# A first balancing round with its row maximum subtracted and 1e-9 added to its column sums

## The chip, the core and the metric

The kernel runs on one core of one Trainium2 chip. The metric is the device time of one execution in microseconds (us). A core has five engines that run their own instruction lists and wait for one another by semaphores: TensorE (PE in the profile, its weight loads PEld), VectorE (DVE), ScalarE (ACT), GpSimd (POOL) and SyncE (SP). Transfers between the device memory and the core's SBUF run on 16 DMA engines and are issued by SyncE, ScalarE or GpSimd.

## The reference

Attention over blocks with a learned order of the blocks, and then a two-branch feed-forward. What matters here is the head: a matrix of 8 x 8 for each of 4 batches and 8 heads is balanced in five rounds (Sinkhorn), and mixes the blocks of k and v.

```python
P = sort_net                                   # [4, 8, 8, 8]
for _ in range(5):
    P = P - np.max(P, axis=-1, keepdims=True)
    P = np.exp(P)
    P = P / (np.sum(P, axis=-1, keepdims=True) + 1e-09)
    P = P / (np.sum(P, axis=-2, keepdims=True) + 1e-09)
...
k_sorted = np.einsum('bhij,bhjcd->bhicd', P, k_b)
v_sorted = np.einsum('bhij,bhjcd->bhicd', P, v_b)
...   # scores within each block of 96 rows, softmax, times v_sorted -> x [3072, 512]
h1 = x @ w1
h2 = x @ w2
out = np.maximum(h1, h2) @ w_out               # [3072, 512]
```

The sequence has 768 rows, the head dimension is 64, w1 and w2 are 512 x 1024, w_out is 1024 x 512; the inputs and the output are float32.

## The kernel before

**The list of steps.** The whole work of four batches is written as a list of short tokens, which is read from left to right and emits instructions (`token`, L1081, and `plan`, L1176). Each engine executes its own instructions in that order, so the list is a schedule made by hand: a step that waits on an engine holds back everything that stands later in the list on the same engine. The list begins

```
lw1 lw2 I1 lk0.0 lk0.1 lk0.2 lq0.0 lq0.1 lq0.2 S0 m0 S1 m1 S2 m2 tv0.18A S3 tv18.36A lq0.3
J1 S4 m3 tv36.56A tv56.80A D0 ...
```

`lw`, `lk` and `lq` issue loads of v, k and q from GpSimd; `I1` makes the identity `ident` on GpSimd; `S0` to `S4` are the five balancing rounds; `m0` to `m2` make masks on VectorE between the rounds and `m3` copies them on GpSimd; `tv` turns v on ScalarE; `J1` makes selection matrices on GpSimd (`one_j`, `sel_v`), as `g1` to `g3` do (`sel_k`, `sel_v`); `D0` spreads the balanced matrix over the partitions (`block_diagonals_first`, L357).

**The rounds.** `sort_net` is loaded by SyncE into `p_sb`, 32 partitions (batch x head) of 8 x 8 float32 (L115). A round, `sinkhorn` (L269), is one Exp on ScalarE in place (L270) and six VectorE instructions in place: row sums into `rowsum` (L276), their reciprocal (L277), a product with the reciprocal spread along the row (L278), column sums into `colsum` (L281), their reciprocal (L282), and the product (L283), which in the last round writes `p_bf` in bfloat16. There is no maximum and no 1e-9 in any of the five rounds. Each instruction needs the one before it.

**TensorE meanwhile.** From the start TensorE multiplies zeros (`keep_streaming`, L78): 92 matmuls of 118 columns (L1079). In rounds 3 and 4 it multiplies zeros again, six matmuls of 512 columns each, with weights `late` that VectorE sets to zero in that round behind the round before it (`late_zeros`, L86 to L88), so that these matmuls start with the round. 

**Behind the rounds.** `D0` is nine small matmuls with `p_bf` (L361, L368); with their results VectorE makes the block-diagonal weights `bd` (L376 to L393), with which TensorE sorts k (L489) and v (L510) of batch 0. Then come scores (L584), Exp (L599), values (L612), and the feed-forward, which is computed by block sums and differences (`sums_x`, `sums_g`, L891, L907; products at L805 and L961), with the later batches' attention in between. `x` is turned by DMA transposes from SBUF to SBUF for batches 1 to 3 (L642). Loads for the later batches and the weights are issued by GpSimd in the order of the list.

Of the kernel before, what the change touches and what calls it, by code (L numbers as in the profile page):

```python
# [16 lines left out]
def kernel(  # L17
# [16 lines left out]
    nc = tc.nc  # L34
    AF = mybir.ActivationFunctionType
    ALU = mybir.AluOpType
    AX = mybir.AxisListType

    B, H, S, D = q.shape
    NB = sort_net.shape[-1]  # L40
    BLK = S // NB
    G = B * H
# [24 lines left out]
    def ps_f32(name):  # L67
        return psum.tile([128, 1024], FP32, tag="ps", name=name)
# [9 lines left out]
    def keep_streaming(ps, n, by=None, most=512):  # L78

        w0 = fill[:, 0:128] if by is None else late[by]  # L80
        while n > 0:
            w = min(n, most)
            nc.tensor.matmul(ps[:, 0:w], w0, fill[:, 0:w], start=True, stop=True)  # L83
            n -= w

    def late_zeros(by):  # L86
        late[by] = const.tile([128, 128], BF16, tag=f"late{by}", name="late")
        nc.vector.memset(late[by], 0.0)  # L88
# [25 lines left out]
    p_sb = const.tile([G, NB, NB], FP32, tag="p_sb", name="p_sb")  # L114
# [150 lines left out]
    rowsum = const.tile([G, NB], FP32, tag="rowsum", name="rowsum")  # L265
    colsum = const.tile([G, NB], FP32, tag="colsum", name="colsum")
    p_bf = const.tile([G, NB, NB], BF16, tag="p_bf", name="p_bf")

    def sinkhorn(it, meanwhile=None):  # L269
        nc.scalar.activation(out=p_sb, in_=p_sb, func=AF.Exp)  # L270
        if meanwhile:
            meanwhile()
        if it >= 3:
            late_zeros(it)
            keep_streaming(ps_f32("fill_ps"), 3072, it)
        nc.vector.reduce_sum(out=rowsum, in_=p_sb, axis=AX.X)  # L276
        nc.vector.reciprocal(out=rowsum, in_=rowsum)  # L277
        nc.vector.tensor_tensor(  # L278
            out=p_sb, in0=p_sb, in1=rowsum.to_broadcast([G, NB, NB]), op=ALU.mult
        )  # L280
        nc.vector.reduce_sum(out=colsum, in_=p_sb.transpose([0, 2, 1]), axis=AX.X)  # L281
        nc.vector.reciprocal(out=colsum, in_=colsum)  # L282
        nc.vector.tensor_tensor(  # L283
            out=p_bf if it == 4 else p_sb,
            in0=p_sb,
            in1=colsum.to_broadcast([G, NB, NB]).transpose([0, 2, 1]),
            op=ALU.mult,
        )
# [792 lines left out]
    def token(text):  # L1081
# [8 lines left out]
        elif kind == "J":  # L1090
            first_selections()
        elif kind == "S":
            sinkhorn(n[0])
        elif kind == "m":
            masks(n[0]) if n[0] < 3 else spread_masks()
# [141 lines left out]
```

## Time and profile before

| | |
|---|---|
| runs | 155.61, 155.71, 156.41 us, median 155.71 us |
| the profiled execution | 156.11 us, of which the span from the first to the last instruction is 154.3 us |
| busy share of the span | TensorE 96%, VectorE 87%, ScalarE 66%, GpSimd 16% |
| granted TensorE clock | 1.00 over the span |
| chain that ended last | TensorE 62%, VectorE 24%, ScalarE 4%, DMA 3%, issue 3% |

The profile is one execution. The timeline's rows have the start and the length in us, counted from the span's start, then engine, line of the kernel, operation, output <- inputs, and the shape with the type; "x3" is three instructions in one row, and the bracket tells how long the engine was idle before and what ended that. The chain that ended last is followed back from the last instruction, at each step to what released it. A busy share is a mean over stages with different limits.

### The profile page before, as it was taken

Reading aid. Unit: us, or ns where it says so; the run is one execution under the profiler, and the core shown is the slowest. Engines: PE = TensorE matmul, PEld = TensorE weight load, DVE = VectorE, ACT = ScalarE, POOL = GpSimd, SP = SyncE. Lnnn points to the kernel's source line nnn. Section 1 sums busy time; section 2 is a strip of 40 time slices with the busy share of each in tenths; the row PEclk is TensorE's granted clock in tenths of the full one; section 3 lists DMA queues with packets and bytes.
Section 4 is the critical chain, followed back from the end, with each engine's and each line's share of the span. In section 5 each row is a group of like instructions: output and inputs, shape, how many; then the busy total and the mean of one; then the engine's idle time right before and its main releaser. Section 6 shows DMA issues by size and latency. Waiting matters only on the chain.

```text
span 154.3 us, 5157 instructions
## 1 busy us (share of the span) xinstructions
PE 147.4 (96%) x2238; PEld 114.0 (74%) x2238; DVE 134.7 (87%) x287; ACT 102.0 (66%) x134; POOL 25.3 (16%) x53
## 2 busy tenths in 40 slices
PE   6999989999999999999999999989999999999991
PEld 6948867555678788887567998765688978578881
DVE  4888989999999999986999999658899999999731
ACT  3488897268899997879859797888792301463010
POOL 7999541100210400001500000000000000000000
PEclk9999999999999999999999999999999999999999
DMA  3999999999999972998999939996001475500065
GB/s 45 197 207 197 197 204 207 217 215 215 216 215 199 205 155 57 150 133 219 287 205 211 188 62 150 165 195 253 0 4 24 85 116 203 187 6 0 0 224 184
DMA packets 28918, 23.93 MB, mean 155 GB/s; under 512 B 16672, under 2 KB 24608, under 8 KB 28896
## 3 DMA queue, kind: packets, MB, share of 16 engines
q0 software_dynamic: 9280, 13.37, 49.1%
q1 hardware_dynamic: 19200, 9.84, 28.9%
q10 hardware_dynamic: 416, 0.39, 0.8%
q8 instruction: 17, 0.28, 0.7%
q14 instruction: 5, 0.04, 0.1%
HBM read 26.75 MB, written 6.29 MB: 214 GB/s over the span
## 4 chain that ended last, share of the span: by engine, by line
PE 62%; DVE 24%; ACT 4%; DMA 3%; issue 3%; DVEq 0%
PE out_ps L961 32%; PE hb_ps L805 10%; PE hq_ps L805 8%; PE o_ps L612 4%; DVE g L824 4%; DVE x L629 3%; PE k_ps L489 3%; PE s_ps L584 3%; DMA xT<-x 2%; ACT kT L109 2%; DVE w_sb L771 2%; PE v_ps L554 1%; DVE v_dc L255 1%; DVE sums_x L891 1%; DVE w_sb L236 1%
## 5 line engine op out<-in xcount | busy, mean ns | idle before, releaser
L805 PEld LDWEIGHTS <-w_sb 128*128 128x128 bf16 x224 | 21.5, 98 | 14.7 <-issue 0.8
L599 ACT ACTIVATE e<-s_ps 96x768 bf16<-96x768 f32 x32 | 24.1, 807 | 2.2 <-PE s_ps L584 2.0
L629 DVE TENSOR_TENSOR x<-o_ps,rs 96x512 bf16<-96x512 f32 x32 | 22.0, 686 | 1.1
L996 ACT COPY o<-out_ps 128x512 f32<-128x512 f32 (+1 forms) x18 | 8.6, 479 | 21.5 <-PE out_ps L961 21.2
L961 PEld LDWEIGHTS <-g 128*128 128x128 bf16 x192 | 18.2, 98 | 2.4
L805 PE MATMUL hb_ps<-sums_x,w_sb 128*128 128x384 bf16 x96 | 18.2, 327 | 0.0
L961 PEld LDWEIGHTS <-sums_g 128*128 128x128 bf16 x144 | 13.5, 97 | 2.2 <-issue 0.2
L961 PE MATMUL out_ps<-wo_sb,g 128*128 128x256 bf16 x96 | 13.1, 273 | 0.0
L987 DVE TENSOR_TENSOR o<-out_ps,o 128x512 f32<-128x512 f32 (+1 forms) x16 | 8.9, 553 | 4.7 <-PE out_ps L961 4.6
L109 ACT CAST kT<-k_ps 128x1024 bf16<-128x1024 f32 x12 | 11.6, 1020 | 2.0 <-PE k_ps L489 2.0
L805 PE MATMUL hq_ps<-xT,w_sb 128*128 128x384 bf16 x64 | 12.7, 326 | 0.0
L612 PE MATMUL o_ps<-v_sb,e 96*128 96x65 bf16 x256 | 12.4, 194 | 0.0
L612 PEld LDWEIGHTS <-e 96*128 96x128 bf16 x256 | 10.7, 98 | 1.5 <-DVE x L629 0.2
L961 PE MATMUL out_ps<-w2T,sums_x 128*128 128x256 bf16 x72 | 11.8, 273 | 0.0
L584 PE MATMUL s_ps<-qT,kT 64*128 64x96 bf16 x256 | 9.2, 204 | 1.1 <-ACT qT L109 0.7
L111 DVE CAST v_sb<-v_ps 96x1024 bf16<-96x1024 f32 x8 | 9.6, 1214 | 0.2 <-PE v_ps L531 0.2
L961 PEld LDWEIGHTS <-sums_x 128*128 128x128 bf16 x96 | 8.6, 97 | 1.2
L584 PEld LDWEIGHTS <-kT 64*128 64x128 bf16 x256 | 6.4, 94 | 3.5 <-issue 2.6
L826 ACT ACTIVATE g<-g 128x768 bf16<-128x768 bf16 x7 | 5.9, 842 | 4.4 <-DVE g L824 4.4
L83 PE MATMUL fill_ps<-fill 128*128 128x118 bf16 x92 | 7.3, 264 | 1.2 <-DVE fill L74 1.2
L176 POOL DMA_DIRECT2D v_raw<-in_v_dram x11 | 6.5, 597 | 11.2 <-DVE v_dc L255 4.3
L109 ACT CAST v_sb<-v_ps 96x1024 bf16<-96x1024 f32 x8 | 7.8, 1016 | 0.6 <-PE v_ps L554 0.6
(129 smaller groups left out, 304.2 us busy)
## 6 DMA issues: line engine op xcount, KB each, us to landing
out_dram<-o SPq DMA_DIRECT2D x10, 512.0 KB, 2.9
v_raw<-in_v_dram POOLq DMA_DIRECT2D x8, 384.0 KB, 16.2
k_raw<-in_k_dram POOLq DMA_DIRECT2D x3, 768.0 KB, 10.8
w_sb<-in_moe_w_dram POOLq DMA_DIRECT2D x4, 256.0 KB, 7.6
wo_sb<-in_moe_w_out_dram POOLq DMA_DIRECT2D x2, 512.0 KB, 11.2
w_sb<-in_moe_w_dram POOLq DMA_DIRECT2D x2, 512.0 KB, 14.8
v_raw<-in_v_dram POOLq DMA_DIRECT2D x3, 256.0 KB, 4.7
k_raw<-in_k_dram POOLq DMA_DIRECT2D x3, 256.0 KB, 6.4
```

The costliest lines, as they stand in the source:

```text
L83: nc.tensor.matmul(ps[:, 0:w], w0, fill[:, 0:w], start=True, stop=True)
L109: nc.scalar.copy(out=out_ap, in_=in_ap)
L111: nc.vector.tensor_copy(out=out_ap, in_=in_ap)
L176: nc.gpsimd.dma_start(out=v_raw[r0 : r0 + 64, m * n : (m + 1) * n], in_=v_src[b, :, m * n : (m + 1) * n],)
L584: nc.tensor.matmul(ps[:, h2 * 512 + ii * 128 : h2 * 512 + ii * 128 + BLK], kT[b][rows, (hp * 8 + i) * BLK : (hp * 8 + i) * BLK + 128], rhs ...
L599: nc.scalar.activation(out=e_out, in_=src, func=AF.Exp, scale=scale)
L612: nc.tensor.matmul(ps[:, h2 * 512 + ii * 65 : h2 * 512 + (ii + 1) * 65], e[:, (h2 * 4 + ii) * BLK : (h2 * 4 + ii) * BLK + 128], v_sb[:, m0 ...
L629: nc.vector.tensor_tensor(out=x, in0=ov[:, :, :, 0:D], in1=rs.to_broadcast([BLK, 2, 4, D]), op=ALU.mult,)
L805: nc.tensor.matmul(ps[:, m * 512 : m * 512 + TCH], w[:, k, c : c + 128], x[:, k], start=new and k == 0, stop=k == 1, skip_group_check=True,)
L961: ins = nc.tensor.matmul(self.ps[:, bank * 512 + p * NW : bank * 512 + (p + 1) * NW], left(self.b, lw, k, ti * 128), right(rw, k), start=n ...
L987: ins = nc.vector.tensor_tensor(out=self.part(ch, half), in0=self.by_tile(self.bank(n)), in1=other, op=ALU.add)
L996: ins = nc.scalar.copy(out=out, in_=self.by_tile(self.bank(n)))
```

## The change

In round 0 alone the row maximum is taken and subtracted ahead of the Exp, and 1e-9 is added to the column sums ahead of their reciprocal. `rowsum` holds the maxima until the row sums overwrite it. The row sums of round 0, and rounds 1 to 4, are computed as before, and the list of steps is the same.

```diff
     def sinkhorn(it, meanwhile=None):
+        if it == 0:
+            nc.vector.reduce_max(out=rowsum, in_=p_sb, axis=AX.X)
+            nc.vector.tensor_tensor(
+                out=p_sb, in0=p_sb, in1=rowsum.to_broadcast([G, NB, NB]), op=ALU.subtract
+            )
         nc.scalar.activation(out=p_sb, in_=p_sb, func=AF.Exp)
         if meanwhile:
             meanwhile()
@@ -279,6 +284,10 @@
             out=p_sb, in0=p_sb, in1=rowsum.to_broadcast([G, NB, NB]), op=ALU.mult
         )
         nc.vector.reduce_sum(out=colsum, in_=p_sb.transpose([0, 2, 1]), axis=AX.X)
+        if it == 0:
+            nc.vector.tensor_scalar(
+                out=colsum, in0=colsum, scalar1=1e-9, scalar2=None, op0=ALU.add
+            )
         nc.vector.reciprocal(out=colsum, in_=colsum)
```

## The prediction, made before the changed kernel ran

> **What bounds the kernel now.** I read the page's chain that ended last first, then the chain piece by piece in order of time, then the waits of the engines, and last the timeline of the first 13 us. The page gives the shares of that chain by engine:
>
> ```profile
> PE 62%; DVE 24%; ACT 4%; DMA 3%; issue 3%; DVEq 0%
> ```
>
> Seen as a whole the kernel is a TensorE kernel with a VectorE stretch. But an average over the span says nothing about the place that is changed. The change sits in the balancing rounds, which run from the landing of `sort_net` to `p_bf`, and those rows of the chain in order of time (start, length, what) read:
>
> ```profile
> 0.75 1.72 DMA p_sb<-in_sort_net_dram
> ...
> 11.76 0.36 PE pe L361 x8
> ...
> 12.47 0.71 PE k_ps L489 x32
> ...
> 13.20 2.84 ACT kT L109 x3
> ...
> 20.93 0.21 DVE rs L623
> ```
>
> From the landing at 0.75 + 1.72 = 2.47 us every piece up to 11.76 us is a step of the rounds (VectorE, with ScalarE's Exp between); then TensorE spreads `p_bf` over the partitions, sorts k, and ScalarE, then VectorE, take over. So in this stage the bound is a chain of tiny dependent instructions, and the tensor work that makes up the rest of the kernel cannot begin until it has ended. The question is whether a later start of all this would be caught up. That would need a place downstream that waits for something with a fixed arrival, a load from memory above all. The list of waits (engine, tile and line, what it waited for: us in total, times, longest) has only three rows in which VectorE, TensorE or ScalarE waits for a DMA:
>
> ```profile
> DVE sums_x L891 <- DMA xT<-x: 2.3, 1, 2.3
> ...
> PE hb_ps L805 <- DMA xT<-x: 0.6, 1, 0.6
> ...
> ACT p_sb L270 <- DMA p_sb<-in_sort_net_dram: 0.5, 1, 0.5
> ```
>
> Two are for the on-chip transposes of `x`, which are issued when VectorE has made `x`, and so move with the work; the third is `p_sb` itself. No computing engine waits for a load of q, k, v or a weight. A delay at the head should therefore reach the end in full, neither shrunk nor grown.
>
> **The change part by part.** Nothing is removed or reordered; in round 0 alone three VectorE instructions come in. Round 0 and the start of round 1 on the timeline (start, us, engine, line, operation, tiles, shape):
>
> ```profile
> 2.49 0.26 ACT L270 ACTIVATE p_sb<-p_sb 32x64 f32<-32x64 f32 x1 [0.46 <-DMA p_sb<-in_sort_net_dram]
> 2.77 0.21 DVE L276 TENSOR_REDUCE rowsum<-p_sb 32x8 f32<-32x64 f32 x1 [0.86 <-ACT p_sb L270]
> ...
> 3.02 0.19 DVE L277 RECIPROCAL rowsum<-rowsum 32x8 f32<-32x8 f32 x1
> 3.21 0.29 POOL masks.py:199 TENSOR_SCALAR_AFFINE_SELECT ident<-ident 128x128 bf16<-128x128 bf16 x1
> 3.24 0.33 DVE L278 TENSOR_TENSOR p_sb<-p_sb,rowsum 32x64 f32<-32x64 f32 x1
> 3.45 1.64 POOL L167 DMA_DIRECT2D k_raw<-in_k_dram  x3
> 3.61 0.25 DVE L281 TENSOR_REDUCE colsum<-p_sb 32x8 f32<-32x64 f32 x1
> 3.90 0.19 DVE L282 RECIPROCAL colsum<-colsum 32x8 f32<-32x8 f32 x1
> 4.12 0.21 DVE L283 TENSOR_TENSOR p_sb<-p_sb,colsum 32x64 f32<-32x64 f32 x1
> ...
> 4.37 0.26 ACT L270 ACTIVATE p_sb<-p_sb 32x64 f32<-32x64 f32 x1 [1.62 <-DVE p_sb L283]
> ...
> 5.12 0.21 DVE L278 TENSOR_TENSOR p_sb<-p_sb,rowsum 32x64 f32<-32x64 f32 x1
> 5.37 0.25 DVE L281 TENSOR_REDUCE colsum<-p_sb 32x8 f32<-32x64 f32 x1
> ```
>
> *The maximum.* A reduction of 32x64 to 32x8 along the last axis has its twin in L276: 0.21 us, and the instruction that needs it starts 3.02 - 2.77 = 0.25 us after it. It takes the place of the Exp as the one that waits for the landing. Ahead of it on VectorE are only the memsets that open the kernel; behind it is nothing that anyone needs sooner than round 0's own work. So +0.25 us, all of it on the path.
>
> *The subtraction.* A 32x64 operation with a broadcast 32x8 operand is L278's form. That row has two prices here, 0.33 us at 3.24 and 0.21 us at 5.12, with 0.37 and 0.25 us to the next start. GpSimd explains the difference below; between 2.74 and 2.95 us its select (at 3.21) has not begun, so I take the short one. From such an operation to the Exp behind it is 4.37 - 4.12 = 0.25 us, so +0.25 us, and Exp starts near 2.99 instead of 2.49 us.
>
> *The 1e-9.* An addition to 32x8 float in place has no row. The nearest by size and place is the reciprocal of the same tile, L282: 0.19 us, and 4.12 - 3.90 = 0.22 us to the next start. It lies beside GpSimd's issue of the k loads (3.45 to 5.09 us) and isn't stretched. I take +0.22 us. The nearest by operation is the tensor-scalar of L828:
>
> ```profile
> L828 DVE TENSOR_SCALAR g<-g x17: 359/360/554, 38.0 to 138.9; 128x768 bf16<-128x768 bf16 x17
> ```
>
> Its least and its median are 0.36 us (the columns are least, median and longest in ns); the longest took 0.55. The timeline shows it beside a load that GpSimd issues:
>
> ```profile
> 45.53 0.90 POOL L153 DMA_DIRECT2D k_raw<-in_q_dram  x1 [4.54 <-PE k_ps L489]
> ...
> 46.03 0.55 DVE L828 TENSOR_SCALAR g<-g 128x768 bf16<-128x768 bf16 x1
> ```
>
> So one end for the addition is 0.22 us and the other 0.22 + (0.55 - 0.36) = 0.41 us. It can't gain by itself: it is one more dependent step.
>
> Together +0.25 + 0.25 + 0.22 = +0.72 us, if all other steps kept their length. They don't, since GpSimd's instructions up to 10.8 us run on a clock of their own and the VectorE steps slide past them. Rounds 3 and 4, with GpSimd's copies between:
>
> ```profile
> 8.53 0.30 POOL L226 COPY one_j<-ident 32x128 bf16<-32x128 bf16 x1
> 8.64 0.27 DVE L278 TENSOR_TENSOR p_sb<-p_sb,rowsum 32x64 f32<-32x64 f32 x1
> ...
> 9.13 0.33 POOL L1068 COPY maskJ<-maskJ 128x16 f32<-128x16 f32 x2
> ...
> 9.41 0.28 POOL L218 COPY sel_k<-ident 32x128 bf16<-32x128 bf16 x1
> 9.46 0.30 DVE L283 TENSOR_TENSOR p_sb<-p_sb,colsum 32x64 f32<-32x64 f32 x1
> ...
> 10.00 0.28 POOL L218 COPY sel_k<-ident 32x128 bf16<-32x128 bf16 x1
> ...
> 10.55 0.39 DVE L278 TENSOR_TENSOR p_sb<-p_sb,rowsum 32x64 f32<-32x64 f32 x1
> 10.59 0.28 POOL L218 COPY sel_k<-ident 32x128 bf16<-32x128 bf16 x1
> 10.82 3.07 POOL L195 DMA_DIRECT2D w_sb<-in_moe_w_dram  x4
> 10.98 0.26 DVE L281 TENSOR_REDUCE colsum<-p_sb 32x8 f32<-32x64 f32 x1
> ```
>
> The two-input operations are stretched exactly where GpSimd runs a copy or a select: 0.33 us beside the select at 3.21, 0.27 beside the copies at 8.53, 0.30 beside 9.41, 0.39 beside 10.59; beside the issue of a load (4.12 us) they take 0.21. Reductions and reciprocals are not stretched in any of these rows.
>
> The Trainium skill, SBUF — State Buffer, section "Who interferes with whom", states this as a rule: a VectorE instruction with two SBUF inputs contends with a GpSimd instruction that reads SBUF, not with one that only writes, a reduction never does, and the loser waits. The trace agrees, with the rows just named. The same section speaks against the change at another point: a tensor-scalar may enter a mode that takes both ports and then contends with any GpSimd instruction, a load's issue included, which the second rival below prices from rows.
>
> With the new starts, round 0's L278 moves to 3.24 + 0.50 = 3.74 us, past the select's end at 3.50: 0.37 becomes 0.25, so -0.12. From there everything is 0.38 later, and from the addition on 0.60 later. Round 3's L278 comes at 9.24 (beside the copies at 9.13) and its L283 at 10.06 (beside 10.00): both keep a GpSimd copy beside them, so I leave their 0.27 and 0.30 us; their bounds are 0.21 and 0.39 us each, so together -0.15 to +0.21. Round 4's L278 comes at 10.55 + 0.60 = 11.15 us, when GpSimd only issues loads (from 10.82): 10.98 - 10.55 = 0.43 becomes 0.25, so -0.18.
>
> Sum: +0.72 - 0.12 - 0.18 = **+0.42 us** at `p_bf`, with bounds 0.42 - 0.15 = +0.27 and 0.42 + 0.21 + 0.19 = +0.82. TensorE's first use moves from 11.76 to about 12.2 us, and by the chain the end moves with it: the profiled execution, 156.11 us of which the span is 154.3, would become 156.53. The median of the runs shown is 155.71, which is 0.40 below that execution, so on the scale of the medians **156.1 us**. The three runs shown spread from 155.61 to 156.41, and 0.5%, 0.78 us here, is about what a measurement of this kernel can tell from no change: the sum lies inside it.
>
> **The rivals.** First, *TensorE loses its pace in the new pause* (the one on the slow side). The opening fill and the late zeros stand thus:
>
> ```profile
> 1.20 7.25 PE L83 MATMUL fill_ps<-fill 128*128 128x118 bf16 x92 [1.20 <-DVE fill L74]
> ...
> 8.00 0.11 DVE L88 MEMSET late<- 128x64 uint32 x1
> ...
> 8.24 1.01 PEld L83 LDWEIGHTS <-late 128*128 128x128 bf16 x6
> ...
> 9.90 1.47 PE L83 MATMUL fill_ps<-fill,late 128*128 128x512 bf16 x6 [0.15 <-DVE late L88]
> ```
>
> The last row ends at 11.37 us and becomes about 11.97, still ahead of 12.2, so the late zeros don't become what arrives last; what could matter is the pause. The opening fill ends at 8.45 us whatever VectorE does, while the weights of the late fill come with the memset, which moves from 8.00 to 8.60. Its loads then start near 8.84 instead of 8.24: a pause of about 0.4 us, where there was none. In the table of one-microsecond windows, of the opening fill alone (window, its length, TensorE busy and count, weight loads busy and count, granted clock, DMA share, GB/s), the pace of one and the same matmul nearly doubles while the clock column stays at 1.00:
>
> ```profile
> 3.00:4.00 1.00, 1.00 (x13) 1.00 (x11) 1.00 0.83 135
> ...
> 7.00:8.00 1.00, 1.00 (x24) 1.00 (x21) 1.00 1.00 186
> ```
>
> If the pause brought back the slow pace, the tensor pieces on the chain behind it, 0.36 + 0.71 = 1.07 us, would grow by 24/13 - 1 = 0.85 of themselves, 0.91 us: +1.33 in all, 157.0 us. The point from which it decides is a pause long enough to bring the slow pace back. Against it: the kernel already has a pause of 0.39 us, from 11.37 to 11.76, and the 32 matmuls behind it take 0.71 us, 22 ns each, so they are not visibly slow. The Trainium skill, TensorE: Matmul & The Clock Gate, Part 1, puts the return to the slow state at an idle window of about 3.4 us; by that rule the rival is dead, though no run here shows how long a pause it takes.
>
> Second, *the addition is held by GpSimd*. It would start near 3.90 + 0.38 = 4.28 us, in the middle of three issues that take 1.64 us, 0.55 each. Held by 0.19 us as in the L828 row, the sum is +0.61 (156.3 us); held for a whole issue, +0.97 (156.7 us). It is over 0.5% once it is held for more than 0.36 us. For it: the operation is L828's. Against: eight elements are little, and the reciprocal in that place wasn't held. The Trainium skill's rule (SBUF — State Buffer, the section above) is that the loser waits for the other's whole instruction; here that would be to the end of the second issue, estimated at 3.45 + 2 x 0.55 = 4.55 us, so 0.27 us and 156.4 us. The L828 row only half agrees: it was held 0.19 us although the load's issue went on for 0.40 us after its start.
>
> Third, *the delay is caught up downstream*, by a wait that the profile credits to another cause: 155.7 us. For it: the loads are issued early by GpSimd at its own pace. Against: the three rows of waits above.
>
> A gain by over 0.5% would need a stage that runs 0.78 us and more faster for starting later; only the contention with GpSimd could do that, and all of it in the rounds is worth 0.12 + 0.18 + 0.15 = 0.45 us, less than the instructions cost.
>
> **How the numbers follow.** Forecast as summed: 0.50, of which 0.07 lies above 0.5%, when the upper bounds meet (+0.82), and 0.05 is for a knock-on in the hand-made order that makes the delay grow. Addition held: 0.20, split 0.09 within and 0.11 above 0.5%. Pace lost: 0.14, slower. Caught up: 0.11, no difference. A gain by something not seen: 0.05. So slower 0.07 + 0.05 + 0.11 + 0.14 = 0.37; faster 0.05; within 0.5% 0.38 + 0.09 + 0.11 = 0.58. The range reaches from the caught-up case, 155.7, to the lost pace, 157.0; the gain and what goes beyond 157.0 are left out.
>
> **What would show it.** In the changed profile: a reduction first after the landing, Exp near 2.99 us; round 0's second two-input step at 0.21 instead of 0.33 us; the addition at 0.19 us (held: 0.3 or more); round 4's L278 row at 0.21 instead of 0.39; the first spreading matmul near 12.2 us; every later row of the chain later by the same amount. A slow fill or longer k-sorting matmuls would show the first rival; a shift at 12 us that is gone by the end would show the third. I am wrong if the shift at the first spreading matmul lies outside +0.27 to +0.82, or if the shift at the end differs from it by more than 0.3 us.

## The result, and the profile after

| kernel | runs | median us | range |
|---|---|---|---|
| before | 20 | 155.73 | 155.26 to 156.51 |
| changed | 20 | 156.62 | 155.94 to 159.5 |

The measured ratio is 1.005, with a 95% interval of 1.0032 to 1.0067: 0.50 to 1.04 us slower, around the bound of 0.5%; it leaves out the one slow run, of 159.5 us at a mean granted clock of 0.978. The medians themselves differ by 0.89 us. The forecast was 156.1 us, in a range of 155.7 to 157.0.

The profiled execution of the changed kernel is not a typical one. It took 158.14 us (span 156.3), 1.5 us above the median, at a mean granted clock of 0.989. These lines of its page answer to the share line of before (40 slices of the span, the granted clock in tenths; the chain's shares; the queue that carries instructions: packets, MB, share):

```profile
PEclk9999978999999999999999999999999999999999
...
q8 instruction: 17, 0.28, 0.7%
...
PE 58%; DVE 28%; ACT 5%; issue 4%; DMA 3%; DVEq 0%
```

The 7 and the 8 in the clock line are a dip near 22 us, far behind the change; it comes back below. At the head, the timeline of the same execution:

```profile
2.30 0.21 DVE L271 TENSOR_REDUCE rowsum<-p_sb 32x8 f32<-32x64 f32 x1 [0.38 <-DMA p_sb<-in_sort_net_dram]
2.54 0.21 DVE L272 TENSOR_TENSOR p_sb<-p_sb,rowsum 32x64 f32<-32x64 f32 x1
2.79 0.26 ACT L275 ACTIVATE p_sb<-p_sb 32x64 f32<-32x64 f32 x1 [0.76 <-DVE p_sb L272]
...
3.54 0.21 DVE L283 TENSOR_TENSOR p_sb<-p_sb,rowsum 32x64 f32<-32x64 f32 x1
...
4.07 0.16 DVE L288 TENSOR_SCALAR colsum<-colsum 32x8 f32<-32x8 f32 x1
4.27 0.19 DVE L291 RECIPROCAL colsum<-colsum 32x8 f32<-32x8 f32 x1
...
8.54 1.47 PE L83 MATMUL fill_ps<-fill,late 128*128 128x512 bf16 x6 [0.88 <-DVE late L88]
...
9.79 0.32 DVE L292 TENSOR_TENSOR p_sb<-p_sb,colsum 32x64 f32<-32x64 f32 x1
...
10.90 0.21 DVE L283 TENSOR_TENSOR p_sb<-p_sb,rowsum 32x64 f32<-32x64 f32 x1
...
11.93 0.36 PE L370 MATMUL pe<-p_bf,one_j 32*128 32x8 bf16 x8 [0.21 <-DVE p_bf L292]
```

The maximum to the subtraction takes 0.24 us, the subtraction to Exp 0.25, the addition to the reciprocal 0.20: 0.69 together. Round 0's product with the reciprocal row sums (3.54) and round 4's (10.90) take 0.21 us. All of this is as forecast, except that `sort_net` is waited for only to 2.30 us and not to 2.49, so Exp starts at 2.79, and the first spreading matmul is at 11.93, only 0.17 later than in the profile before. The head has to be read from the landing on: first use of `p_sb` to first spreading matmul took 11.76 - 2.49 = 9.27 us before, and 11.93 - 2.30 = 9.63 here, +0.36.

The chain in order of time goes on as before, piece by piece of the same length and later:

```profile
0.75 1.52 DMA p_sb<-in_sort_net_dram
...
11.93 0.36 PE pe L370 x8
...
12.63 0.70 PE k_ps L498 x32
...
13.36 2.84 ACT kT L109 x3
```

The list of waits has the rows for `x` and `sort_net` as before, and one that was not there, a wait of TensorE for a load:

```profile
DVE sums_x L900 <- DMA xT<-x: 2.3, 1, 2.3
...
PE hb_ps L814 <- DMA xT<-x: 0.6, 1, 0.6
DVE rowsum L271 <- DMA p_sb<-in_sort_net_dram: 0.4, 1, 0.4
PEld L498 <- DMA k_raw<-in_k_dram: 0.3, 1, 0.3
```

The end of this execution is 2.03 us late. Where that comes in shows on TensorE, in the rows behind the widest pause near 20 us, of the changed kernel and then of before:

```profile
20.77 0.35 PE L593 MATMUL s_ps<-qT,kT 64*128 64x96 bf16 x8 [1.15 <-ACT e L608]
```

```profile
20.20 0.35 PE L584 MATMUL s_ps<-qT,kT 64*128 64x96 bf16 x8 [0.75 <-ACT qT L109]
```

The pause is longer (1.15 against 0.75 us) and the same scores start 0.57 us later. The clock follows, in windows of 3.4 us (length, busy time and count of TensorE, then of its weight loads, VectorE, ScalarE and GpSimd, then granted clock, DMA share, GB/s), of the changed kernel and of before:

```profile
18.10:21.50 3.40, 2.25 (x62) 1.86 (x58) 2.62 (x3) 2.73 (x4) 1.25 (x3) 1.00 1.39 202
21.50:24.90 3.40, 3.40 (x48) 2.68 (x46) 2.47 (x5) 2.62 (x4) 0.79 (x2) 0.50 1.25 209
```

```profile
18.10:21.50 3.40, 2.65 (x65) 2.29 (x64) 2.99 (x5) 3.13 (x5) 1.22 (x3) 1.00 1.39 199
21.50:24.90 3.40, 3.40 (x79) 2.71 (x76) 3.33 (x8) 3.38 (x5) 1.08 (x2) 1.00 1.24 208
```

At half clock TensorE does 48 matmuls in the second window instead of 79. Matched instruction by instruction on VectorE, the execution is 0.57 us late at 20.9 us, 1.95 at 50 us, and 2.03 at the end. So 0.17 of the 2.03 us comes from the start of the spreading, 0.40 from the longer pause and some 1.4 from the window at half clock. But of all 30 runs of the changed kernel (with the repeats below) only 2 have a mean clock under 0.993, so the median can't come from that, and the first question was what a typical execution looks like.

### The profile page after: what moved, and what is told of

The parts are those of the page before. It is cut to its first block, busy times and chain, and to the rows that moved or that the text cites. A ratio compares the mean times of both kernels' runs of the same rounds, so it can differ in the third digit from the quotient of the medians.

```text
span 156.3 us, 5160 instructions
## 1 busy us (share of the span) xinstructions
PE 148.1 (95%) x2238; PEld 114.1 (73%) x2238; DVE 135.3 (87%) x290; ACT 102.2 (65%) x134; POOL 25.8 (16%) x53
## 4 chain that ended last, share of the span: by engine, by line
PE 58%; DVE 28%; ACT 5%; issue 4%; DMA 3%; DVEq 0%
PE out_ps L970 32%; PE hb_ps L814 7%; DVE g L833 6%; PE hq_ps L814 5%; PE o_ps L621 5%; PE s_ps L593 3%; PE k_ps L498 3%; DVE sums_x L900 3%; DMA xT<-x 2%; DVE x L638 2%; DVE v_dc L255 2%; ACT kT L109 2%; DVE w_sb L780 1%; PE v_ps L563 1%; DVE g L837 1%
## 5 line engine op out<-in xcount | busy, mean ns | idle before, releaser
L814 PEld LDWEIGHTS <-w_sb 128*128 128x128 bf16 x224 | 21.5, 98 | 14.7 <-issue 0.8
L250 ACT COPY v_dc<-v_raw 64x1152 bf16<-64x1152 bf16 (+3 forms) x6 | 8.2, 1379 | 0.0
```

What stands on the lines that cost most here:

```text
L250: nc.scalar.copy(out=dst.rearrange("p (d c two) -> p d c two", c=BLK, two=2)[:, :, c0:c1], in_=src.rearrange("p (c d two) -> p d c two", c ...
L814: nc.tensor.matmul(ps[:, m * 512 : m * 512 + TCH], w[:, k, c : c + 128], x[:, k], start=new and k == 0, stop=k == 1, skip_group_check=True,)
```

## The experiments

Two theories stood at first. *The head*: three dependent instructions lengthen it by their sum, and what they relieve by sliding past GpSimd is less than forecast. *The instruction blocks*: the pause near 20 us is TensorE waiting for its own next instructions, which come by DMA (17 packets in the page), so a later start changes that wait, and with it the clock. From the second round of runs on, a third: *the race*, that the relief depends on when `sort_net` lands, since GpSimd's copies run on fixed times.

**1. The changed kernel again**, no edit.

> The changed kernel once more, for a second profile of it. Theory D (the delay of the rounds is carried to the end as it is): +0.36 to 0.42 us at the first spreading matmul, counted from the landing of sort_net, and the same at the end, so a median near +0.4 us (ratio 1.003). Theory I (TensorE's instruction stream is fetched by DMA in blocks of 256 instructions, a fetch that is asked for a little later queues behind more of the loads, and TensorE stands at its 702nd instruction for it): the pause near 19.8 us is 1.1 to 1.3 us again, where the kernel before has 0.82, and the median is +0.8 to 0.9 us. Theory C (the granted clock falls to one half for a window of 3.4 us because of the longer pause): the profile shows a clock of 0.989 again and a median of +1.5 us or more; with a clock of 1.00 it explains nothing of the median.

Measured: 156.62 us against 156.06, 1.0039 (1.0023 to 1.0056). Its profile (156.76 us, clock 1.00) is a typical one. Timeline:

```profile
2.44 0.21 DVE L271 TENSOR_REDUCE rowsum<-p_sb 32x8 f32<-32x64 f32 x1 [0.53 <-DMA p_sb<-in_sort_net_dram]
...
3.22 0.29 POOL masks.py:199 TENSOR_SCALAR_AFFINE_SELECT ident<-ident 128x128 bf16<-128x128 bf16 x1
...
3.68 0.21 DVE L283 TENSOR_TENSOR p_sb<-p_sb,rowsum 32x64 f32<-32x64 f32 x1
...
4.22 0.16 DVE L288 TENSOR_SCALAR colsum<-colsum 32x8 f32<-32x8 f32 x1
...
11.98 0.28 PE L370 MATMUL pe<-p_bf,one_j 32*128 32x8 bf16 x5 [0.22 <-DVE p_bf L292]
```

The head is 9.54 us, with no stretched product in it. The pause near 20 us is back at its old length, and no dip follows (timeline of TensorE):

```profile
20.45 0.35 PE L593 MATMUL s_ps<-qT,kT 64*128 64x96 bf16 x8 [0.78 <-ACT qT L109]
```

So the longer pause and the dip aren't what makes the median slower.

**2. The instruction blocks moved.** The opening fill in 124 narrower matmuls instead of 92, the same columns in all, which puts 64 more instructions (a weight load and a matmul each) ahead on TensorE.

```diff
-    keep_streaming(ps_f32("fill_ps"), 92 * 118, most=118)
+    keep_streaming(ps_f32("fill_ps"), 92 * 118, most=88)
```

> The changed kernel, with its opening fill of the same 10856 columns cut into 124 matmuls of 88 columns instead of 92 of 118: 64 more TensorE instructions ahead of everything, the same work behind. D: nothing changes, +0.4 us against the kernel before, and the pause near 19.8 us stays. I: the boundary between two fetched blocks moves from instruction 702 to what was 638 before, ahead of the scores that wait for ScalarE's qT copy in any case, and its fetch is asked for some 1.5 us sooner: the pause near 19.8 us falls to 0.4 us or less, and the end comes 0.5 to 1.0 us earlier than that of the changed kernel, -0.3 to +0.3 us against the kernel before.

Measured: 158.63 us, 1.0142 (1.0109 to 1.0175); four of the six runs have a mean clock of 0.966 to 0.989. TensorE on the timeline:

```profile
19.58 0.56 PE L519 MATMUL v_ps<-bd,v_dc 64*128 64x64 bf16 x14 [1.21 <-DVE v_sb L111]
...
20.86 0.34 PE L593 MATMUL s_ps<-qT,kT 64*128 64x96 bf16 x8
```

The pause has moved from ahead of these scores to the products of v that stand before them. By number it stayed: it lies within two places of TensorE's 702nd instruction, as in all profiles but the two of experiment 7. That much of the theory is shown: the pause belongs to the instruction's number, not to the data. In the trace of each of the fourteen profiles a packet of the instruction queue ends 1.4 to 1.6 us before TensorE starts that instruction (before: 18.60 and 20.20; changed: 19.31 and 20.77; this kernel: 18.17 and 19.58). The gain expected from moving it failed, though: now v's products come late, VectorE waits for them before it can cast them, and the kernel is 2 us slower than the changed one. Not all of that is this pause: matched on VectorE with the first profile of before, this execution is 0.24 us late when the spreading begins, 1.05 at 20.9 us and 2.25 at the end. The pause accounts for 0.8 us; where the other 1.2 come from isn't shown.

**3. Each half alone.** The changed kernel without the 1e-9, and without the maximum and the subtraction:

```diff
-        if it == 0:
-            nc.vector.tensor_scalar(
-                out=colsum, in0=colsum, scalar1=1e-9, scalar2=None, op0=ALU.add
-            )
```

> Only the maximum and the subtraction of round 0, without the 1e-9. At the first spreading matmul +0.50 less 0.12 and 0.18 us for the contention with GpSimd that goes: +0.2 us from the landing. D: +0.2 us at the end. I: +0.2 to 0.8 us at the end, depending on what the pause near 19.8 us makes of it.

```diff
-        if it == 0:
-            nc.vector.reduce_max(out=rowsum, in_=p_sb, axis=AX.X)
-            nc.vector.tensor_tensor(
-                out=p_sb, in0=p_sb, in1=rowsum.to_broadcast([G, NB, NB]), op=ALU.subtract
-            )
```

> Only the 1e-9 on round 0's column sums. The addition 0.16 us long, +0.20 us to the next start, not held by GpSimd; with round 4's product still partly beside GpSimd's copy, +0.1 to 0.2 us at the first spreading matmul. D: the same at the end. I: +0.1 to 0.6 us at the end, with the pause near 19.8 us.

Measured: 156.37 us (1.002, 0.9999 to 1.0042) and 156.26 us (1.0015, 0.9995 to 1.0034). Over the 156.06 us of before, on the same chip, that is +0.31 and +0.20, and +0.56 for both together (experiment 1). In us the halves add up about as their instructions do (two and one), but either interval still touches no change; alone they would decide nothing.

**4. Before again**, no edit.

> The kernel before against itself, for a second profile of it and for what the measurement tells from no change. Every theory: a ratio of 1.000 within 0.002. The question is its transposes near 100 us: in the first profile of it the last one took 3.65 us from issue to landing, in three profiles of changed kernels 3.92 to 4.16. If a second profile of it shows 3.9 or more, the late part of the difference is the spread between executions (D); if it shows 3.7 or less, the late part belongs to the change.

Measured: 156.13 us against 156.11, 1.0009 (0.999 to 1.0029). Timeline:

```profile
2.35 0.26 ACT L270 ACTIVATE p_sb<-p_sb 32x64 f32<-32x64 f32 x1 [0.32 <-DMA p_sb<-in_sort_net_dram]
...
3.10 0.21 DVE L278 TENSOR_TENSOR p_sb<-p_sb,rowsum 32x64 f32<-32x64 f32 x1
3.22 0.29 POOL masks.py:199 TENSOR_SCALAR_AFFINE_SELECT ident<-ident 128x128 bf16<-128x128 bf16 x1
...
10.17 0.21 DVE L278 TENSOR_TENSOR p_sb<-p_sb,rowsum 32x64 f32<-32x64 f32 x1
...
11.20 0.36 PE L361 MATMUL pe<-p_bf,one_j 32*128 32x8 bf16 x8 [0.21 <-DVE p_bf L283]
```

The 9.27 us head of the first profile isn't typical. `sort_net` landed 0.14 us earlier, round 0's product with the reciprocal row sums started at 3.10, ahead of GpSimd's select at 3.22 (in the first profile at 3.24, behind the select at 3.21), and took 0.21 instead of 0.33 us; from there every step ran ahead of GpSimd's copies, none of the four products that were stretched in the first profile (0.33, 0.27, 0.30, 0.39 us) was stretched here, and the head is 11.20 - 2.35 = 8.85 us. Undisturbed against undisturbed, the change costs 9.54 - 8.85 = 0.69 us, the plain sum of the three instructions. The question put ahead of the run stays undecided by its own measure: the last transposes of `x` took 3.81 us, between the 3.7 and the 3.9 named.

**5. The addition three and seven times**, to measure what a delay at the head is worth at the end. The kernel with three has `range(2)`, the one with seven `range(6)`.

```diff
+            for _ in range(2):
+                nc.vector.tensor_scalar(
+                    out=colsum, in0=colsum, scalar1=1e-9, scalar2=None, op0=ALU.add
+                )
```

> The changed kernel with its addition three times in a row: two more dependent instructions of 0.20 us to the next start, +0.40 us at the head (0.7 to 0.8 us against the kernel before). D: the end moves by the same, +0.4 us against the changed kernel, ratio 1.005 to 1.008 with it. I: the pause at TensorE's 702nd instruction grows with the delay of the request, so +0.4 to 0.9 us. C: more executions with a granted clock under 0.995.

> The same with the addition seven times: +1.2 us at the head against the changed kernel, +1.5 to 1.6 against the kernel before. D: +1.5 to 1.9 us at the end, ratio 1.010 to 1.012, so a slope of one. I: a slope over one, +2 us or more, because the fetch for the 702nd instruction then queues behind the loads that GpSimd issues at 13.9 to 16.4 us as well. If loads caught the delay up, the slope would fall below one here first.

Measured: 157.16 us (1.0063, 1.0041 to 1.0086) and 158.53 us (1.0144, 1.0119 to 1.0169), so +0.54 and +1.91 over the 156.62 us of the changed kernel. The heads in their profiles are 10.13 and 11.27 us, +0.59 and +1.73 over experiment 1. What is added to the head arrives at the end, about one for one. Over the 156.11 us of before measured beside them it is +1.05 and +2.42 us; the second is more than was expected of a delay that passes on in full (1.010 to 1.012) and lies in what was expected of the instruction blocks (+2 us or more). But the pause at the 702nd instruction was 0.76 us, no longer than elsewhere; what had grown was the head, by 1.73 and not by 1.2 us. Timeline of the kernel with seven:

```profile
4.18 0.16 DVE L288 TENSOR_SCALAR colsum<-colsum 32x8 f32<-32x8 f32 x1
4.37 1.62 DVE L292 TENSOR_SCALAR colsum<-colsum 32x8 f32<-32x8 f32 x6
5.07 1.45 POOL L153 DMA_DIRECT2D q_raw<-in_q_dram  x2
6.03 0.19 DVE L295 RECIPROCAL colsum<-colsum 32x8 f32<-32x8 f32 x1
```

The seven take 6.03 - 4.18 = 1.85 us, 0.26 each, where one alone takes 0.20 to the next start. One by one they are 0.160, 0.193, 0.160, 0.305, 0.159, 0.476 and 0.159 us: three of them are longer, and each of these three ends within 0.02 us of the end of the load issue that runs beside it on GpSimd (issues that end at 4.58, 5.11 and 5.81 us). The other four began in the first 0.15 us of an issue and weren't held. The second rival's mechanism exists.

**6. The weights' loads held back**, to see whether the fetch of instructions queues behind data. GpSimd copies one column of `kT`, which it must wait for, before it issues the loads of `w_out`.

```diff
+        elif kind == "e":
+            nc.gpsimd.tensor_copy(out=landed[:, 3:4], in_=kT[0][:, 32:33])
...
-        a3.0 T3D s0.2 v0.4 s0.7 T1D v0.0 x0.2A v0.7 a3.1 c0.0 w0.1D a1.2.4 v0.2 v0.6 v0.3 w0.3D
+        e0 a3.0 T3D s0.2 v0.4 s0.7 T1D v0.0 x0.2A v0.7 a3.1 c0.0 w0.1D a1.2.4 v0.2 v0.6 v0.3 w0.3D
```

> The changed kernel, with one tiny GpSimd copy that reads the last third of kT (made by 16.2 us) ahead of the two loads of w_out, so that these 1 MB are issued some 2.3 us later. I: the fetch of the block that holds the 702nd instruction, asked for near 14.9 us, finds only the loads of w2 ahead of it; it starts by 17 us instead of 18, and the pause there falls from 0.85 to 0.3 to 0.5 us, VectorE's first reciprocal near 21.2 us comes 0.3 us earlier. The end is open, since w_out then lands later and its first product at 25.4 us may wait. If the pause has nothing to do with the loads, it stays at 0.8 us and more.

Measured: 156.53 us, 1.0022 (1.0004 to 1.0039), not distinguishable from the changed kernel. GpSimd on the timeline:

```profile
16.54 0.19 POOL L1140 COPY landed<-kT 128x1 bf16<-128x1 bf16 x1 [2.65 <-ACT kT L109]
16.77 1.48 POOL L188 DMA_DIRECT2D wo_sb<-in_moe_w_out_dram  x2
```

The two loads are issued 2.7 us later than in the changed kernel (14.04 and 14.11 us in its first two profiles), but the packet with the instructions came no earlier (18.36 to 19.33 us), the pause was 0.90 us, and the DMA engines stayed as busy with the loads issued before. So it isn't shown that the fetch waits for data loads. This profile also has the one single addition that was held, 0.25 instead of 0.16 us; `sort_net` landed late (2.53 us), and so it began late beside GpSimd's second load of k, whose issue ran from 4.02 to 4.57 us:

```profile
4.31 0.25 DVE L288 TENSOR_SCALAR colsum<-colsum 32x8 f32<-32x8 f32 x1
```

**7. Two loads of q exchanged**, in both kernels. In experiment 4 the spreading started 0.56 us earlier than in the first profile, but at 15.6 us only 0.22 was left. TensorE's weight loads there wait for q. If the last load of q that it waits for is a fixed arrival, then the exchange shows it.

```diff
-        lw1 lw2 I1 lk0.0 lk0.1 lk0.2 lq0.0 lq0.1 lq0.2 S0 m0 S1 m1 S2 m2 tv0.18A S3 tv18.36A lq0.3
+        lw1 lw2 I1 lk0.0 lk0.1 lk0.2 lq0.0 lq0.2 lq0.1 S0 m0 S1 m1 S2 m2 tv0.18A S3 tv18.36A lq0.3
```

> The kernel before, with the second and the third load of q exchanged in GpSimd's order, so that the first q transposes near 14.2 us wait for a load that lands some 0.7 us later. Theory Q (where the rounds end early, TensorE waits for q, and part of the new instructions' time falls into that wait): TensorE waits for q_raw for 0.3 to 1.0 us and the kernel is 0.2 to 0.8 us slower than before. D (no load is ever waited for): no difference.

> The changed kernel with the same exchange. Q: its rounds end 0.7 us later, the q load lands when it did, so that the wait is 0.6 to 0.7 us shorter than in the other exchanged kernel and the change costs 0.0 to 0.4 us between the two, less than the 0.6 to 0.8 us between the kernels as they are. D: it costs the same 0.6 to 0.8 us between the two.

Measured: 156.28 us (1.0004, 0.9982 to 1.0025) and 156.62 us (1.0027, 1.001 to 1.0045). TensorE's weight loads for q: before without the exchange (experiment 4), before with it, changed with it:

```profile
14.79 0.36 PEld L436 LDWEIGHTS <-q_raw 128*64 128x64 bf16 x12 [0.28 <-DMA q_raw<-in_q_dram]
```

```profile
15.52 0.36 PEld L436 LDWEIGHTS <-q_raw 128*64 128x64 bf16 x12 [1.02 <-DMA q_raw<-in_q_dram]
```

```profile
15.40 0.36 PEld L445 LDWEIGHTS <-q_raw 128*64 128x64 bf16 x12 [0.20 <-DMA q_raw<-in_q_dram]
```

With the exchange the spreading starts at 11.22 us in before and at 11.92 in the changed kernel, 0.70 apart; before waits 1.02 us for q and the changed kernel 0.20; and at 20.9 us both stand equal (+0.02 and +0.01 us against the first profile). A head that is early enough runs into q's landing. The medians of the two still differ by 0.34 us, within the 0.0 to 0.4 expected if q's landing counts, but before with the exchange is not distinguishable from before without it, where 0.2 to 0.8 us more was expected. So with one profile of each it stays open how much of what is caught up there is kept to the end.

In the list as it is, q's landing is not what ends last. In experiment 4 ScalarE's copy of the turned q starts 0.56 us earlier than in the first profile of before, in spite of the 0.28 us of waiting for q, and the scores behind it only 0.23 us earlier (experiment 4, and then the copy of the first profile, whose scores started at 20.20 us):

```profile
17.61 1.44 ACT L109 COPY qT<-tq_ps 128x1536 bf16<-128x1536 bf16 x1
...
19.97 0.35 PE L584 MATMUL s_ps<-qT,kT 64*128 64x96 bf16 x8 [0.73 <-ACT e L599]
```

```profile
18.17 1.44 ACT L109 COPY qT<-tq_ps 128x1536 bf16<-128x1536 bf16 x1
```

VectorE had lost 0.34 us of its lead at q by then, but what these scores wait for is something else: between the copy and the scores lies the pause at the 702nd instruction. Its packet ended at 18.55 us here and at 18.60 in the first profile, and TensorE went on 1.42 and 1.60 us after that. In all profiles but those of experiment 2 and of before with the exchange, VectorE at 20.9 us is early or late, against the first profile, by just what the 702nd instruction is, to 0.02 us.

**8. One more look at each kernel**, no edit.

> The kernel before, for one more profile. Theory R (the rounds' products race with GpSimd's select and copies, whose times are fixed from the start, while the rounds start with the landing of sort_net): with a landing before 2.46 us the product of round 0 starts before the select at 3.21 us and takes 0.21 us, and the rounds take 8.85 to 9.0 us from the landing to the first spreading matmul; with a later landing the product takes 0.3 us and the rounds 9.0 to 9.3.

> The changed kernel, for one more profile. R: at most one or two of the products of rounds 3 and 4 are stretched, and the rounds take 9.54 to 9.75 us from the landing, whatever the landing is: 0.7 us over the undisturbed rounds of the kernel before.

Measured, one run each: 155.84 and 155.94 us. The heads are 9.08 and 9.66 us. The changed one is like the others. For before I expected an early landing to bring a short head, and the landing was the earliest of all (2.29 us), but one product was stretched (0.30 us), and then TensorE itself was late:

```profile
8.90 2.54 PE L83 MATMUL fill_ps<-fill,late 128*128 128x512 bf16 x11
11.37 0.37 PE L361 MATMUL pe<-p_bf,one_j 32*128 32x8 bf16 x8
```

In the one-microsecond windows of the fills alone (length, TensorE busy and count, weight loads busy and count, clock, DMA share, GB/s) the fast pace comes only at 7 us:

```profile
6.00:7.00 1.00, 1.00 (x13) 1.00 (x12) 1.00 1.05 195
7.00:8.00 1.00, 1.00 (x22) 1.00 (x21) 1.00 1.07 195
```

So the opening fill lasted to 8.85 us, and the late fill ended just as the spreading began. TensorE's pace can also bound the head.

The heads together (us; stretched are products of the rounds over 0.225 us):

| profile | first use of `p_sb` | first spreading matmul | head | stretched |
|---|---|---|---|---|
| before, first | 2.49 | 11.76 | 9.27 | 4 |
| before again | 2.35 | 11.20 | 8.85 | 0 |
| before, one look | 2.29 | 11.37 | 9.08 | 1 |
| before, q exchanged | 2.39 | 11.22 | 8.83 | 0 |
| changed, first | 2.30 | 11.93 | 9.63 | 1 |
| changed again | 2.44 | 11.98 | 9.54 | 0 |
| changed, one look | 2.29 | 11.95 | 9.66 | 2 |
| changed, q exchanged | 2.30 | 11.92 | 9.62 | 1 |
| maximum only | 2.43 | 11.96 | 9.53 | 2 |
| 1e-9 only | 2.42 | 11.81 | 9.39 | 3 |
| loads held back | 2.53 | 12.20 | 9.66 | 1 |

The mean head is 9.01 us in the four profiles of before, and 9.61 in the first four of the changed kernel: +0.60. Over all runs of these comparisons the changed kernel's median is 156.62 (30 runs) and that of before 156.05 (104 runs): +0.57 us.

## Why the prediction was right, and where it was not

**The three instructions: right.** +0.25, +0.25 and +0.22 were forecast; the rows show 0.24, 0.25 and 0.20, and undisturbed heads differ by 0.69. The addition took 0.16 us, not 0.19.

**The relief of 0.12 + 0.18 us: the term that was mis-sized.** Both rows did what was forecast (0.21 us each), but the comparison was with one profile of before, in which the landing at 2.47 us had put round 0's product 0.03 us behind the select's start. Profiles that land 0.10 to 0.20 us earlier have none or one of the four stretches. On the mean heads the relief is 0.69 - 0.60 = 0.09 us, not 0.30. Corrected, the sum would have been some +0.6.

**"No computing engine waits for a load": the step that failed.** For loads of data it held in the profile that was read, and not in others. An early head can wait for q (0.28 us in experiment 4), and k of the last batch is waited for in some executions, early head or not; the kernel with the 1e-9 only, on TensorE's timeline:

```profile
82.64 1.71 PE L493 MATMUL k_ps<-bd,k_raw 64*64 64x64 bf16 x96 [0.31 <-DMA k_raw<-in_k_dram]
```

For instructions it failed even there: the pause of TensorE near 20 us in the first profile, which the timeline puts down to ScalarE's copy of q (0.75 us), ends 1.60 us after a packet of instructions, as it does in the other profiles, and is the wait that ends last in that stage. This is what the third rival named, a wait that the profile credits to another cause, and it is partly true: matched on VectorE at 20.9 us, the two typical profiles of the changed kernel stand at +0.25 and +0.19 against the first profile of before, and its three at 0, -0.23 and -0.18, a difference of 0.36 us where the spreading had 0.52. How much is caught up is up to the packet, which set out 2.9 to 3.5 us after an instruction that the head moves; that scatter is as large as the effect of the change. A head that is later still passes on in full up to there: +0.78 and +1.91 us behind the rounds with three and seven additions are +0.76 and +1.85 at 20.9 us.

**The net.** Forecast +0.42. The medians differ by 0.89 us in the first comparison, by 0.56 in its repeat, and by 0.57 over all runs; the last figure mixes the comparisons, as two thirds of the changed kernel's runs and a fifth of those of before are from the first one. The repeat lies inside the bounds of +0.27 to +0.82; of the first comparison the interval reaches over them and the difference of the medians lies above. The sum took a relief that was too large (by 0.21 us) and a catching-up not at all. The predicted time is 0.52 us under the median that came out, and only 0.21 of that is explained. That the median fell into the range of 155.7 to 157.0 says little for the sum, since the range reaches from no change to the lost pace.

**TensorE's pace in the new pause: not seen.** The pause came, larger than forecast (0.88 us in the changed profile, where 0.4 was expected, since the opening fill, which was taken to end at 8.45 us, ended between 7.44 and 8.93 us in the fourteen profiles, and here at 7.66), and the six matmuls behind it took 1.47 us as before. The clock did fall in that execution, but at 21.5 us behind another pause.

**The addition held by GpSimd: missed by luck.** It took 0.16 us in all profiles of the changed kernel itself, where it began at 4.06 to 4.22 us, and 0.25 in experiment 6, where it began at 4.31. It begins 1.77 to 1.78 us after the first use of `p_sb`, so with the landing of the profile that was read, whose first use was at 2.49 us, it would have begun near 4.27: by an estimate from all the additions recorded (held from 0.24 us behind the start of an issue, not held up to 0.21), just late enough to be held to the end of the issue, for about 0.13 us.

**My own test** asked for the shift at the first spreading matmul to lie within +0.27 to +0.82 and for the end to follow within 0.3 us. Profile by profile both fail (+0.17 at 11.93 us, +2.03 at the end); on the means they hold (+0.60 on the heads, +0.57 in the times of all runs; with the 0.89 of the first comparison the end differs from the heads by 0.29, just inside the 0.3). The test should have been put in heads, not in starts.

**What stays open.** The end of single executions scatters by -0.45 to +0.41 us near the transposes of `x` at 96 to 103 us, in both kernels; their piece in the chain is 3.65, 3.81, 3.85 and 4.05 us long in the profiles of before, and 3.76, 3.87, 3.87 and 3.99 in those of the changed kernel. These overlap, so no part of the difference is shown to come from there; nor is it shown why 0.36 us at 20.9 us reads 0.56 and more in the times. Open too is whether the change makes the dip of the clock more frequent: a mean under 0.993 has 2 of 30 runs against 1 of the 84 of before whose clocks are listed.

## What to carry to other kernels

A relief that comes from two engines passing each other by hundredths of a us belongs to the execution, not to the kernel: look at the distance between the two rows, and where it is smaller than the scatter of the landing ahead of them, take the undisturbed price and keep the rest for the range. "Nobody waits for a load" is likewise true of a profile; ask by how much each load is early, and check the wait that ends last in the stage against the packets of instructions, before calling a delay uncaught. And before a changed profile is explained, compare its own time with the median: here it was 1.5 us off, by a cause that the median doesn't share.

## What the runs showed of the hardware

Instructions came during the run, in 17 packets of 0.28 MB together, 16 KB each; that they are TensorE's, and that it waits for them, is read from how its pause follows them in all profiles. In twelve of the fourteen profiles TensorE stood still for 0.76 to 1.28 us, from one start to the next, within two places of its 702nd instruction (in the two of experiment 7 up to 0.44 us), and moving the number moved the pause to other work. It is in before as well (0.82 us), and typically the change leaves it as it is (0.85). The packet that ends it set out 2.9 to 3.5 us after TensorE's 463rd instruction, wherever that stood (13.97 us in experiment 2, 16.58 with seven additions); what holds it so long wasn't found.

The clock fell to half for 3.41 us (21.52 to 24.94) after a window of 3.40 us in which TensorE was busy for 2.25 us; with 2.62 us, in experiment 1, it did not fall. The Trainium skill, TensorE: Matmul & The Clock Gate, Part 1, speaks of an idle window of about 3.4 us. The length agrees with this trace; but here the clock fell behind a window that was idle for only about a third, in one execution, and experiment 2's, busy for 1.89 us, was followed by full clock:

```profile
18.10:21.50 3.40, 1.89 (x50) 1.58 (x45) 2.19 (x3) 2.81 (x4) 1.33 (x3) 1.00 1.41 200
21.50:24.90 3.40, 3.38 (x79) 2.70 (x79) 3.33 (x8) 3.18 (x5) 1.09 (x2) 1.00 1.24 207
```

So neither the busy time of a window cut at these places nor the pause alone decides it.

VectorE's products of 32x64 beside a GpSimd copy or select have a plain rule: each of the 20 that took 0.225 us or more in the first 14 us of the fourteen profiles (0.21 us undisturbed) ended 0.07 to 0.09 us after the end of such an instruction, even where it had started 0.01 to 0.04 us ahead of it (10.55 us, beside the copy at 10.59, in the first profile). So its length is set by where the copy ends.

A tensor-scalar of eight elements was held by 0.02 to 0.32 us beside GpSimd's load issues, or not at all. The five that were held began 0.24 us or more behind the start of an issue, and ended with it, to 0.02 us; those that began up to 0.21 us behind the start took 0.16 us.
